# Block-sparse attention and a two-layer MLP on one core: one shared tile for the far keys of the first and last 32 queries, K copies on three engines, finer steps, another order

## Chip, cores, metric

One core of one Trainium2 chip. The metric is device time in microseconds (us). TensorE is PE, its weight loads PEld, VectorE DVE, ScalarE ACT, GpSimd POOL, SyncE SP.

## What is computed

q, k and v are [4, 8, 768, 64] (batch, heads, sequence, head size), in float32. The 768 positions are 24 blocks of 32.

```python
scores = 0.125 * q @ k^T
mask   = |block_i - block_j| <= 1, or block_i or block_j is 0 or 23,
         or block_j in sampled_blocks[block_i]          # 3 random blocks per row block
attn   = softmax(where(mask, scores, -1e9))
x      = (attn @ v) as [3072, 512]                      # batch*seq, heads*64
h      = x @ w_in                                       # [512, 2048]
g      = h if h >= 1; 0 if h <= -1; else (h + 1)**2 / 4
out    = g @ w_out                                      # [2048, 512]
```

Query blocks 0 and 23 see all keys; every other block sees block 0, block 23, its own, its two neighbours and three sampled ones, 8 blocks or 256 keys (repeats masked by a zero V row).

## The kernel before

**Attention.** Two heads (e = 0, 1) make a pair; there are 4 batches of 4 pairs, written P(b, j). A pair has up to four rounds (`ROUNDS`, line 36). Rounds 1 to 3 hold 8 query blocks, two groups g of four; a block w of a group fills 32 partitions, its 256 keys the columns. Blocks 0 and 23 sit in round 1 with keys 0 to 255; the other 512 keys of these two blocks are round 0. Before the change round 0 is a full tile per head: the block list (0, 1, 2, 23) for both groups, of which only positions 0 and 3 are used later. Per round and head: `scores` (L295) into a PSUM bank, `top` (reduce_max, L306), `expo` (L323, L326), `turn` (four transposes, L332), `turn_copy` (L336, to SBUF as pt), `values` (L350), and per round `norm`. Round 0 is first copied out by `stash` (L300), since its exponential waits for the maximum over both rounds (`top_global`, L311 to L315). float32 scores and values show as two PE instructions per matmul.

**Gathers.** Sampled K blocks are copied in SBUF to kg, three 32-column copies per query block (`gather_k_sampled`, L238): on POOL, in the early ("wide") rounds those with slot 0 (`KD`) on DVE. The block numbers come from registers that an engine loads at its first use (`blocks`, L122). Sampled V blocks go to vb: the first of three by a DMA that SP issues (L261), two by POOL copies (L263) out of va, a pair's near V rows.

**MLP.** `wi` (w_in) and `w` (w_out) are turned from 64-bit words into two float32r parts by 16 conversions: `load` (raw, L167, one buffer), `size` (ACT, L172), `bits` (four DVE operations, L177 to L182), `high` (ACT, L74), `low` (DVE, L191). Conversions 8 to 15 are w_in, 0 to 7 w_out; w_out's parts are kept in DRAM and loaded again later (L455). Each half batch (8 in all) runs 16 steps fi: `l1` (L471 to L473) into h, Relu and Square (L477, L480), max (L483), `gh` (L74), `gl` (L492), `l2` (L499 to L501) into three banks oa, copied out by `o_copy` (L508).

**Order.** Every step is a function in one list, `plan`. The steps get due times from constants, but then `RANK` (line 576), a list with one number per step, replaces them: the steps are issued in its order, and with that the order on each engine and on SP's DMA queue. Rounds 0 to 2 of batch 0 come first, together with the w_in conversions ("wide": up to three spare banks); its round 3 and the pairs of batches 1 to 3 are mixed into the MLP. The first `l1` is at 132 us, the last value matmul at 767 us.

`TCOPY = (1,)`: for the later rounds ACT copies pt of head 1, DVE that of head 0. `TCOPYW = (0,)`: in the wide rounds ACT copies that of head 0. `GL1`: the fi of the first half whose gl POOL makes. `SUBP`: conversions whose `low` POOL makes.

Of the kernel before, what the change touches and what calls it, by code (L numbers as in the profile page):

```python
# [30 lines left out]

ROUNDS = (
# [8 lines left out]
def body(ctx, tc, qk_t, v_rows, v_near, v_last, sampled_blocks, moe_w_in, moe_w_out, near, ident, out):  # L41
# [39 lines left out]
    wi = cst.tile([128, 4, 2, FF], F32R, name="wi")  # L81

# [31 lines left out]

    def blocks(engine, which, i):

        if engine not in held:
            rows = [1] if engine is ENG.SP else [0] if engine is ENG.DVE else [0, 1]
            held[engine] = {}
            for w in rows:  # L120
                for i0 in range(0, NI, 11):
                    _, vals = nc.values_load_multi_w_load_instructions(  # L122
                        kv_at[:, i0:i0 + 11, w], engines=[engine], min_val=0, max_val=2 ** 15 - 1,
                        skip_runtime_bounds_check_because="three fields of five bits, packed on the chip")
                    for k, v in enumerate(vals):
                        held[engine][w, i0 + k + 1] = v
        return held[engine][which, i]
# [80 lines left out]
    def pair(b, j, s, q, wide, rounds=(0, 1, 2, 3)):  # L208
# [21 lines left out]
        def gather_k_sampled(r):  # L230
            kg, kt = gat.tile([128, 8, BLK * NR], F32, name="kg"), st["k"]
            st["kg", r] = kg
            for k0, i0, n in runs(r):
                for k in range(n):
                    eng, et = (nc.vector, ENG.DVE) if wide and k in KD else (nc.gpsimd, ENG.Pool)
                    v = blocks(et, 0, i0 + k)
                    for a in range(NR):
                        eng.tensor_copy(out=kg[:, k0 + k, 32 * a:32 * a + 32],  # L238
                                        in_=kt[:, bass.ds(field(v, a, NB - 1) * BLK, BLK)])
# [11 lines left out]
        def gather_v_sampled(r, engine):  # L251
            vb = st["vb", r]
            for k0, i0, n in runs(r):
                for k in range(n):
                    for a in range(NR):
                        if (a in (V_SPW if wide else V_SP)) is not (engine is ENG.SP):
                            continue
                        v = field(blocks(engine, 1, i0 + k), a, NB)
                        dst = vb[32 * a + 32:32 * a + 64, k0 + k]
                        if engine is ENG.SP:  # L260
                            Q_V.dma_start(out=dst, in_=v_near[b, j, BLK:2 * BLK, bass.ds(v, 1)].rearrange("p a d -> p (a d)"))  # L261
                        else:
                            nc.gpsimd.tensor_copy(out=dst, in_=st["va"][32:64, bass.ds(v, 1)].rearrange("p a d -> p (a d)"))  # L263
# [8 lines left out]

        def scores(r):
            for e in range(2):
                st["s", r, e] = bank(f"s{e}", wide, 3 * j + r)
            kt = st["k"]
            for g in range(2):
                for n in range(3 if r else 1):
                    for w in range(4):
                        i = ROUNDS[r][g][w]  # L280
                        for e in range(2):
                            es = slice(64 * e, 64 * e + 64)
                            c0, c1 = (0, 96, 160, 256)[n:n + 2]
                            if r == 0:
                                c0, c1, rhs = 0, 256, kt[es, 256 + 256 * g:512 + 256 * g]
                            elif is_global(r, g, w):
                                rhs = kt[es, c0:c1]
                            elif n == 0:
# [282 lines left out]
KD = (0,)  # L571
# [231 lines left out]
```

## Time and profile before

| | us |
|---|---|
| median of 3 runs | 922.78 (921.85 to 932.03) |
| the profiled execution | 922.26 |
| its span | 920.5 |
| PE busy / weight loads | 820.0 / 692.9 |
| DVE, ACT, POOL busy | 423.8, 408.6, 448.4 |
| mean granted TensorE clock | 0.937 of full |

Busy times are unions within the span; matmuls overlap, so a mean duration times a count exceeds the time that they take. A wait is named by the semaphore that came last. "Idle before" is the time in which the engine stood before that group, and behind the arrow stands what ended it.

### The profile page before, as it was taken

How to read it: one execution, taken by the hardware profiler on the slowest of the kernel's cores; microseconds unless marked ns; L12 is line 12 of the kernel's file. 1: busy time of each engine (PE TensorE's matmuls, PEld its weight loads, DVE VectorE, ACT ScalarE, POOL GpSimd, SP SyncE). 2: the span in 40 equal slices, each digit the busy share in tenths (PEclk: the TensorE clock that was granted, in tenths of full speed). 3: DMA queues.
4: the chain of work that ended last, by engine and by line, in shares of the span. 5: the costliest groups of instructions: out<-in, count | busy, mean ns of one | idle time of the engine just before them, and what ended most of it. 6: DMA issues, size and time to landing. Idle time of an engine off the chain costs nothing.

```text
span 920.5 us, 33588 instructions
## 1 busy us (share of the span) xinstructions
PE 820.0 (89%) x12000; PEld 692.9 (75%) x12000; DVE 423.8 (46%) x925; ACT 408.6 (44%) x800; POOL 448.4 (49%) x1720
## 2 busy tenths in 40 slices
PE   2576377588999999899999989999999999999997
PEld 1355255467788888788888878888888888899896
DVE  5586673566854444334343434434443443222222
ACT  1344343334654544444445435634454443434343
POOL 2999757556766777346373637454746400000000
PEclk7587597688999999999999999999999999999999
DMA  6666757676656365545355535545463313443432
GB/s 226 200 225 203 244 195 283 228 229 206 232 174 238 95 213 169 182 151 175 128 181 195 166 128 184 172 154 189 134 211 131 117 56 130 149 137 127 160 115 103
DMA packets 56955, 159.54 MB, mean 173 GB/s; under 512 B 10579, under 2 KB 21972, under 8 KB 54228
## 3 DMA queue, kind: packets, MB, share of 16 engines
q1 hardware_dynamic: 56788, 157.40, 51.1%
q8 instruction: 94, 1.54, 0.7%
q14 instruction: 73, 0.60, 0.2%
HBM read 142.68 MB, written 14.68 MB: 171 GB/s over the span
## 4 chain that ended last, share of the span: by engine, by line
PE 70%; DMA 16%; DVE 4%; SPq 4%; issue 3%; ACT 3%; POOL 0%; POOLq 0%; DVEq 0%; ACTq 0%
PE oa L499 9%; PE oa L501 8%; PE oa L500 8%; PE h L471 8%; PE h L473 7%; PE h L472 7%; PE o L350 7%; PE s L295 6%; DMA va<-in_v_near_dram 5%; PE t L332 5%; DMA raw<-in_moe_w_out_dram 3%; SPq L261 3%; DMA raw<-in_moe_w_in_dram 2%; DMA w<-wo_dram 1%; DMA out_dram<-ot 1%
## 5 line engine op out<-in xcount | busy, mean ns | idle before, releaser
L263 POOL COPY vb<-va 32x130 f32 x704 | 234.3, 333 | 132.9 <-PE o L350 82.1
L238 POOL COPY kg<-k 128x32 f32 x1008 | 209.4, 242 | 142.2 <-PE s L295 96.8
L499 PE MATMUL oa<-w,gh 128*128 128x512 f32 x384 | 162.1, 422 | 15.4 <-DMA w<-wo_dram 7.1
L471 PE MATMUL h<-xt,wi 128*128 128x384 f32 x448 | 162.7, 363 | 4.7 <-DVE r L483 4.6
L501 PE MATMUL oa<-w,gl 128*128 128x512 f32 x384 | 153.5, 400 | 0.4 <-POOL gl L492 0.4
L500 PE MATMUL oa<-w,gh 128*128 128x512 f32 x384 | 153.1, 399 | 0.2 <-DVE w L191 0.2
L472 PE MATMUL h<-xt,wi 128*128 128x384 f32 x448 | 153.0, 342 | 0.0
L473 PE MATMUL h<-xt,wi 128*128 128x384 f32 x448 | 152.9, 341 | 0.0
L477 ACT ACTIVATE r<-h,half_c 128x384 f32<-128x384 f32 x112 | 65.2, 582 | 170.9 <-PE h L473 170.5
L483 DVE SCALAR_TENSOR_TENSOR r<-r,h 128x384 f32<-128x384 f32 x112 | 61.8, 552 | 155.6 <-ACT r L480 155.3
L471 PEld LDWEIGHTS h<-xt,wi 128*128 128x128 f32 x448 | 85.8, 192 | 16.5 <-DVE r L483 7.1
L499 PEld LDWEIGHTS oa<-w,gh 128*128 128x128 f32 x384 | 73.6, 192 | 29.9 <-issue 6.8
L74 ACT CAST gh<-r 128x384 fp32r<-128x384 f32 x128 | 65.6, 512 | 65.8 <-DVE r L483 61.4
L492 DVE TENSOR_TENSOR gl<-r,gh 128x384 fp32r<-128x384 f32 x124 | 69.4, 561 | 46.4 <-ACT gh L74 46.0
L472 PEld LDWEIGHTS h<-xt,wi 128*128 128x128 f32 x448 | 86.3, 193 | 4.3
L501 PEld LDWEIGHTS oa<-w,gl 128*128 128x128 f32 x384 | 73.3, 191 | 17.9 <-POOL gl L492 0.8
L295 PE MATMUL s<-k,q 64*32 64x96 f32 (+2 forms) x3376 | 74.5, 265 | 13.4 <-DMA k<-in_qk_t_dram 6.0
L473 PEld LDWEIGHTS h<-xt,wi 128*128 128x128 f32 x448 | 86.0, 192 | 0.0
L326 ACT ACTIVATE p<-s,m 128x256 f32<-128x256 f32 x176 | 72.0, 474 | 30.0 <-DVE m L318 29.6
L350 PE MATMUL o<-va,pt 128*32 128x65 f32 x1408 | 66.2, 235 | 20.0 <-ACT pt L336 12.6
L332 PE MATMUL t<-idf,p 128*128 128x128 f32 x464 | 76.0, 288 | 8.4 <-DVE pt L336 3.7
L500 PEld LDWEIGHTS oa<-w,gh 128*128 128x128 f32 x384 | 73.7, 192 | 9.0 <-issue 1.2
(83 smaller groups left out, 1112.5 us busy)
## 6 DMA issues: line engine op xcount, KB each, us to landing
w<-wo_dram SPq DMA_DIRECT2D x112, 512.0 KB, 3.5
va<-in_v_near_dram SPq DMA_DIRECT2D x20, 1625.0 KB, 8.1
raw<-in_moe_w_in_dram SPq DMA_DIRECT2D x16, 512.0 KB, 4.7
raw<-in_moe_w_out_dram SPq DMA_DIRECT2D x16, 512.0 KB, 5.2
wo_dram<-w SPq DMA_DIRECT2D x16, 512.0 KB, 4.6
q<-in_qk_t_dram SPq DMA_DIRECT2D x20, 384.0 KB, 4.0
k<-in_qk_t_dram SPq DMA_DIRECT2D x20, 384.0 KB, 4.5
vn<-in_v_rows_dram SPq DMA_DIRECT2D x16, 390.0 KB, 4.0
```

The costliest lines, as they stand in the source:

```text
L238: eng.tensor_copy(out=kg[:, k0 + k, 32 * a:32 * a + 32], in_=kt[:, bass.ds(field(v, a, NB - 1) * BLK, BLK)])
L263: nc.gpsimd.tensor_copy(out=dst, in_=st["va"][32:64, bass.ds(v, 1)].rearrange("p a d -> p (a d)"))
L295: nc.tensor.matmul(out=st["s", r, e][32 * w:32 * w + 32, 256 * g + c0:256 * g + c1], lhsT=st["q"][es, i * BLK:(i + 1) * BLK], rhs=rhs, sta ...
L326: nc.scalar.activation(out=p[:, 256 * g:256 * g + 256], in_=st["s", r, e][:, 256 * g:256 * g + 256], func=AF.Exp, bias=st["m", r][:, e, g: ...
L332: nc.tensor.transpose(out=t[:, c * 128:(c + 1) * 128], in_=st["p", r, e][:, c * 128:(c + 1) * 128], identity=idf)
L350: nc.tensor.matmul(out=o[32 * w:32 * w + 32, e, gd], lhsT=st["pt", r, e][:, k:k + 32], rhs=rhs, start=start, stop=stop)
L471: nc.tensor.matmul(out=hv, lhsT=wi[:, j, 0, fs], rhs=x[:, 0], start=(j == 0), stop=False)
L472: nc.tensor.matmul(out=hv, lhsT=wi[:, j, 0, fs], rhs=x[:, 1], start=False, stop=False)
L473: nc.tensor.matmul(out=hv, lhsT=wi[:, j, 1, fs], rhs=x[:, 0], start=False, stop=(j == NP - 1))
L499: nc.tensor.matmul(out=o, lhsT=gh[:, ts], rhs=w[:, 0], start=(fi == 0), stop=False)
L500: nc.tensor.matmul(out=o, lhsT=gh[:, ts], rhs=w[:, 1], start=False, stop=False)
L501: nc.tensor.matmul(out=o, lhsT=gl[:, ts], rhs=w[:, 0], start=False, stop=(fi == NF - 1))
```

## The change

- Round 0 becomes one tile for both heads: only blocks 0 and 23 are computed, head 0 in column groups 0 and 3, head 1 in 1 and 2. So one bank, one stash, one reduce over 512 columns, one exponential, one turn and one copy where there were two. In round 1 head 1's blocks are permuted to match (`place`).
- `top_global` uses an additive mask (`other`, 0 or -3e38) in place of operations on 32 partitions.
- `gather_k_sampled` becomes `gather_k` per half round and engine: in the wide rounds slots 0 and 4 on DVE, 1 and 7 on ACT, the others on POOL. `gather_v_sampled` is split in half rounds as well. Registers are loaded in a step of their own, on ACT too.
- `TCOPY = (0, 1)`, `GL1 = (0, 1, 4, 12)`, `SUBP = (7,)`, and a new `RANK` of 3089 numbers (2989 before).

```diff
-    ((0, 1, 2, 23), (0, 1, 2, 23)),
+    ((), ()),
...
+    other = cst.tile([128, 4], F32, name="other")
...
+        nc.vector.memset(other, -3.0e38)
+        for w, eg in enumerate((0, 2, 3, 1)):
+            nc.vector.memset(other[32 * w:32 * w + 32, eg:eg + 1], 0.0)
...
+        def gather_k(r, part, which):
+            if part == 0 and which == 0:
+                new_k(r)
+            eng, et = ((nc.gpsimd, ENG.Pool), (nc.vector, ENG.DVE), (nc.scalar, ENG.Activation))[which]
+            for k, i in slots(r, part):
+                if which != (1 if wide and k in KD else 2 if wide and k in KA else 0):
+                    continue
+                v = blocks(et, 0, i)
+                for a in range(NR):
+                    (eng.copy if which == 2 else eng.tensor_copy)(out=st["kg", r][:, k, 32 * a:32 * a + 32],
+                                                                   in_=st["k"][:, bass.ds(field(v, a, NB - 1) * BLK, BLK)])
...
+        def place(r, e, g, w):
+            if r == 0:
+                return (0, None, None, 3)[w] if e == 0 else (1, None, None, 2)[w]
+            if r == 1 and e == 1:
+                return ((1, 0, 2, 3), (0, 1, 3, 2))[g][w]
+            return w
+
         def scores(r):
-            for e in range(2):
+            kt = st["k"]
+            for e in range(2 if r else 1):
                 st["s", r, e] = bank(f"s{e}", wide, 3 * j + r)
+            if r == 0:
+                for g in range(2):
+                    for w in (0, 3):
+                        for e in range(2):
+                            es, z, i = slice(64 * e, 64 * e + 64), place(0, e, g, w), (NB - 1) * (w // 3)
+                            nc.tensor.matmul(out=st["s", 0, 0][32 * z:32 * z + 32, 256 * g:256 * g + 256],
+                                             lhsT=st["q"][es, i * BLK:(i + 1) * BLK],
+                                             rhs=kt[es, 256 + 256 * g:512 + 256 * g], start=True, stop=True)
+                return
...
         def top_global():
...
+            a, m = st["a"], st["m", 1].rearrange("p e g -> p (e g)")
+            t = pr.tile([128, 5], F32, name="m0")
+            nc.vector.tensor_tensor(out=t[:, 0:4], in0=m, in1=other, op=ALU.add)
+            nc.vector.tensor_copy(out=t[:, 4:5], in_=a)
+            nc.vector.reduce_max(out=a, in_=t, axis=AX.X)
+            nc.vector.scalar_tensor_tensor(out=m, in0=other, scalar=a[:, 0:1], in1=m, op0=ALU.add, op1=ALU.max)
             nc.vector.tensor_single_scalar(out=a, in_=a, scalar=-SCALE, op=ALU.mult)
...
-                at(t - G["gs"], gather_k_sampled, r)
+                for part in range(2):
+                    for which in range(3 if wide else 1):
+                        at(t - G["gs"] + 2.0 * part + 0.01 * which, gather_k, r, part, which)
...
+    for engine, rows in ((ENG.Pool, (0, 1)), (ENG.SP, (1,))) + (((ENG.DVE, (0,)),) if KD else ()) + (((ENG.Activation, (0,)),) if KA else ()):
+        at(TC + 0.1, registers, engine, rows)
...
-KD = (0,)
+KD = (0, 4)
+KA = (1, 7)
...
-GL1 = (0, 4, 8, 12)
-SUBP = ()
-TCOPY = (1,)
+GL1 = (0, 1, 4, 12)
+SUBP = (7,)
+TCOPY = (0, 1)
```

What the new `RANK` does at the places that the prediction names, read by sorting the steps. On SP, ahead of the load of conversion 9: before, 20 gathers of V blocks, then va of pair 1 between them; after, va of pair 1 first, then 10 gathers. Between the loads of conversions 15 and 0: before, 16 gathers, q, k, vn, va and two small loads; after, 8 gathers, va and one small load. On ACT, ahead of size of conversion 9: one pt copy before, two after; on DVE ahead of its bits: none before, one after. From batch 1 on, the places of a pair's steps among the MLP's `l1` and `l2` are nearly the same; the pairs P(2, 0) to P(2, 2) come a little earlier.

## Rows read from the trace of the kernel before

**Rows 1.** Windows by stage: the stretch in us, its length, then busy us (and instructions) of each engine, the granted clock of TensorE as a share of full, the share of the DMA engines, and GB/s.

```profile
0.00:132.00 132.00, 72.44 (x2004) 53.57 (x2004) 88.92 (x216) 51.09 (x90) 94.04 (x331) 0.73 0.65 216
132.00:250.00 118.00, 92.62 (x1140) 76.57 (x1133) 71.26 (x121) 51.10 (x98) 76.23 (x235) 0.84 0.70 235
250.00:740.00 490.00, 479.80 (x7734) 406.65 (x7733) 212.83 (x493) 234.24 (x477) 278.10 (x1156) 0.99 0.50 165
740.00:920.00 180.00, 175.12 (x1134) 156.08 (x1132) 50.82 (x97) 72.19 (x136) 0.00 (x0) 1.00 0.37 125
```

The columns of engines are PE, PEld, DVE, ACT, POOL.

**Rows 2.** What PE waited for from 250 to 740 us: us in total, times, longest.

```profile
PE oa L499 <- DMA w<-wo_dram: 7.1, 4, 3.8
...
PE t L332 <- ACT pt L336: 0.5, 1, 0.5
```

**Rows 3.** Waits of all engines over the whole span, columns as before.

```profile
DVE cva L177 <- ACT cva L172: 45.1, 11, 9.4
...
ACT cva L172 <- DMA raw<-in_moe_w_in_dram: 39.8, 8, 9.0
...
ACT cva L172 <- DMA raw<-in_moe_w_out_dram: 27.7, 6, 8.2
```

**Rows 4.** The chain that ended last: its shares of the span by line, and one piece of it (start us, us).

```profile
by line: PE oa L499 9.3%; PE oa L501 8.3%; PE oa L500 8.2%; PE h L471 7.7%; PE h L473 7.0%; PE h L472 7.0%; PE o L350 6.9%; PE s L295 5.8%; DMA va<-in_v_near_dram 5.0%; PE t L332 4.9%; issue 3.1%; DMA raw<-in_moe_w_out_dram 2.8%; SPq L261 2
...
24.11 7.63 DMA va<-in_v_near_dram
```

**Rows 5.** Timeline of PE around a turn (start us, us, instruction).

```profile
437.58 0.39 PE L501 MATMUL oa<-w,gl 128*128 128x512 f32 x1
437.81 0.60 PE L332 MATMUL t<-idf,p 128*128 128x128 f32 x4
...
438.48 0.39 PE L500 MATMUL oa<-w,gh 128*128 128x512 f32 x1
```

**Rows 6.** Timeline of PE around the round-0 scores of a later pair, and the score instructions at work in the stretch 470.05 to 470.2 and in 470.3 to 470.4 (durations min/median/max in ns, first and last start in us).

```profile
469.44 0.40 PE L500 MATMUL oa<-w,gh 128*128 128x512 f32 x1
469.67 0.40 PE L501 MATMUL oa<-w,gl 128*128 128x512 f32 x1
470.00 1.09 PE L295 MATMUL s<-k,q 64*32 64x256 f32 x32
...
L295 PE MATMUL s<-k,q x8: 400/400/400, 470.0 to 470.0; 64*32 64x256 f32 x8
...
L295 PE MATMUL s<-k,q x16: 376/388/400, 470.0 to 470.3; 64*32 64x256 f32 x16
```

**Rows 7.** Groups of instructions on ACT from 250 to 740 us: line, operation, shapes, count, then busy us, mean ns of one, idle before.

```profile
L477 ACT ACTIVATE r<-h,half_c 128x384 f32<-128x384 f32 x76 | 44.3, 583 | 120.0 <-PE h L473 119.7
L480 ACT ACTIVATE r<-r 128x384 f32<-128x384 f32 x76 | 40.0, 526 | 2.0
L74 ACT CAST gh<-r 128x384 fp32r<-128x384 f32 x76 | 38.9, 512 | 40.6 <-DVE r L483 40.5
L336 ACT COPY pt<-t 128x512 f32<-128x512 f32 x42 | 24.7, 588 | 33.8 <-PE t L332 33.3
L323 ACT ACTIVATE p<-sg,a 128x512 f32<-128x512 f32 x22 | 15.7, 719 | 2.2 <-DVE a L315 2.2
L300 ACT COPY sg<-s 128x512 f32<-128x512 f32 x21 | 11.6, 589 | 7.9 <-PE s L295 7.9
```

**Rows 8.** Groups by shape over the whole span, columns as in the group above.

```profile
L238 POOL COPY kg<-k 128x32 f32 x1008 | 209.4, 242 | 142.2 <-PE s L295 96.8 <-DMA vb<-in_v_last_dram 16.7 <-DMA k<-in_qk_t_dram 13.0
...
L336 DVE COPY pt<-t 128x512 f32<-128x512 f32 x58 | 40.0, 689 | 58.8 <-PE t L332 58.5
...
L306 DVE TENSOR_REDUCE m<-sg 128x2 f32<-128x512 f32 x32 | 20.6, 678 | 5.9 <-ACT sg L300 5.9
...
L238 DVE COPY kg<-k 128x32 f32 x48 | 6.8, 194 | 7.8 <-issue 5.4 <-PE oa L295 2.0
```

**Rows 9.** DVE's register loads (durations min/median/max in ns, first and last start in us).

```profile
L122 DVEq TENSOR_LOAD <-kv_at x2: 2502/2622/2741, 7.3 to 10.1; - x2
```

**Rows 10.** The second conversion: DVE's, ACT's and SP's timelines (start us, us; in brackets the idle time before and what ended it), and the landing times of all raw loads in us.

```profile
38.23 0.71 DVE L177 TENSOR_SCALAR cva<-cva 128x1024 f32<-128x1024 f32 x1 [9.44 <-ACT cva L172]
...
37.07 1.12 ACT L172 ACTIVATE cva<-raw 128x1024 f32<-128x1024 f32 x1 [8.21 <-DMA raw<-in_moe_w_in_dram]
...
31.82 0.84 SPq L167 DMA_DIRECT2D raw<-in_moe_w_in_dram  x2
...
DMA to landing us min/median/max: 3.6/4.7/10.9
```

**Rows 11.** The first w: timelines of SP, DVE and PE, columns as in the group above.

```profile
120.16 5.00 SPq L261 DMA_DIRECT2D vb<-in_v_near_dram  x8
...
137.79 0.83 SPq L167 DMA_DIRECT2D raw<-in_moe_w_out_dram  x2
...
127.50 1.23 DVE L182 SCALAR_TENSOR_TENSOR cva<-raw,cva 128x1024 int32<-128x1024 int32 x1
...
166.70 0.79 PE L499 MATMUL oa<-w,gh 128*128 128x512 f32 x1 [6.14 <-ACT w L74]
```

**Rows 12.** The last operation of bits of all 16 conversions, and the copies of the outputs on ACT (durations in ns, first and last start in us).

```profile
L182 DVE SCALAR_TENSOR_TENSOR cva<-raw,cva x16: 1224/1226/1266, 18.7 to 246.5; 128x1024 int32<-128x1024 int32 x16
...
L508 ACT COPY ot<-oa x23: 570/587/593, 269.4 to 916.9; 128x512 f32<-128x512 f32 x23
```

More of the change, by code (lines that the diff above doesn't have):

```diff
@@ L113, in body, with registers @@
     held = {}
-    def blocks(engine, which, i):
[L117 to L127, printed above, removed]
+    def registers(engine, rows):
+        for w in rows:
+            for i0 in range(0, NI, 11):
+                _, vals = nc.values_load_multi_w_load_instructions(
+                    kv_at[:, i0:i0 + 11, w], engines=[engine], min_val=0, max_val=2 ** 15 - 1,
+                    skip_runtime_bounds_check_because="three fields of five bits, packed on the chip")
+                for k, v in enumerate(vals):
+                    held[engine, w, i0 + k + 1] = v
+    def blocks(engine, which, i):
+        return held[engine, which, i]
     def field(v, a, top):
@@ L228, in runs, with slots, new_k @@
                 k0 += n
[L230 to L239, printed above, removed]
+        def slots(r, part):
+            k0, i0, n = list(runs(r))[part]
+            return [(k0 + k, i0 + k) for k in range(n)]
+        def new_k(r):
+            st["kg", r] = gat.tile([128, 8, BLK * NR], F32, name="kg")
+        def gather_k(r, part, which):
[9 more added lines that the diff above has]
+                                                                   in_=st["k"][:, bass.ds(field(v, a, NB - 1) * BLK, BLK)])
         def load_va():
@@ L249, in gather_v, with gather_v_sampled @@
             Q_V.dma_start(out=vb[0:32, 0:total], in_=v_last[b, j, :, k:k + total])
-        def gather_v_sampled(r, engine):
+        def gather_v_sampled(r, part, engine):
             vb = st["vb", r]
[L253 to L263, printed above, removed]
+            for k, i in slots(r, part):
+                for a in range(NR):
+                    if (a in (V_SPW if wide else V_SP)) is not (engine is ENG.SP):
+                        continue
+                    v = field(blocks(engine, 1, i), a, NB)
+                    dst = vb[32 * a + 32:32 * a + 64, k]
+                    if engine is ENG.SP:
+                        Q_V.dma_start(out=dst, in_=v_near[b, j, BLK:2 * BLK, bass.ds(v, 1)].rearrange("p a d -> p (a d)"))
+                    else:
+                        nc.gpsimd.tensor_copy(out=dst, in_=st["va"][32:64, bass.ds(v, 1)].rearrange("p a d -> p (a d)"))
         def slot(r, g, quarter):
@@ L329, in turn @@
         def turn(r, e):
-            t = st["t", r, e] = bank("t", wide, 7 * j + 2 * r + e)
+            t = st["t", r, e] = bank("t", wide, 6 * j + max(2 * r - 1, 0) + e)
             for c in range(4):
@@ L379, in x_turn @@
         def x_turn(hf):
[L380 removed]
+            t = st["xt", hf] = bank("t", wide, 6 * j + 5)
             for k, (r, n) in enumerate((((1, 0), (2, 0), (2, 1)), ((3, 0), (3, 1), (1, 1)))[hf]):
```

50 lines of the change are left out of this document (23 added, 27 removed), and 301 rows, old and new, of the table RANK.

## The prediction

> **What bounds the kernel now.** I read the windows by stage first [rows 1]; they show two kernels in one. From 250 to 740 us PE is busy 479.8 of 490 us, and 175.1 of 180 us from there on, at a granted clock of 0.99 to 1.00: PE is the bound, and only PE time that goes shortens the run. In the first 250 us PE is busy 165 us (granted clock 0.73, then 0.84), DVE 160 and POOL 170: nothing is full, so waits and the order of the steps set the end. The waits of PE from 250 to 740 us [rows 2] confirm the first half: the longest entry is 7.1 us, for w. For the second half I read the waits of all engines [rows 3]: DVE stood 45.1 us before a conversion's first operation, since ACT's came late, and ACT's own stood 39.8 + 27.7 us for the raw weights. The chain of waits [rows 4] gives the va transfers 5.0% and the raw ones 2.8% and more.
>
> **PE: what goes and what only looks as if it did.** Per pair one of two round-0 tiles goes: four transposes, a stash, a 512-wide reduce, an exponential, a copy of pt, and 16 of 32 score instructions.
>
> Transposes: in the PE-bound stage a block of four stands between an L501 that starts at 437.58 and an L500 at 438.48 [rows 5], 0.90 us. Without a block between, two such steps are 2 x 0.23 = 0.46 us (469.44 to 469.67 is one, [rows 6]). A block costs 0.44 us of PE, not the 1.15 us of four times the page's mean, because matmuls overlap. Eleven pairs have their round 0 after 250 us (22 exponentials of sg, two a pair, [rows 7]), one more shortly before: 12 x 0.44 = 5.3 us. A second way: the chain gives L332 4.9% of 920.5 us [rows 4], 45 us for 512 transposes; 64 of these are 5.6 us. I take 5.3. The first four pairs I leave out, because PE waits there.
>
> Round-0 scores: the count halves and I book nothing. In the block of 32 [rows 6] exactly 8 instructions have started within the first 0.2 us and exactly 16 by 470.4: eight places of the array (two halves of the rows by four groups of columns) run side by side, four deep, 1.09 us or 0.27 us a layer. After the change head 0 uses column groups 0 and 3, head 1 groups 1 and 2: four places, and each still gets two key groups of two passes, four deep again. It is between 0 and half the block, 12 x 0.5 = 6 us of further gain; I take 0, because the depth is counted from the rows.
>
> Value matmuls keep number and shape, and the permuted heads of round 1 still fill four different column groups: 0.
>
> **DVE, ACT, POOL.** A later pair takes from DVE a reduce (0.68 us) and four pt copies (0.69 each), 3.4 us [rows 8]. ACT loses a stash (0.59) and an exponential (0.72) and gains three pt copies net (0.59 each): +0.45 us [rows 7], where it is busy 234 of 490 us. PE covers both: 0; with that cover gone ACT's part would cost 12 x 0.45 = 5 us. The new top_global is five small operations for six; its 5-wide reduce, which no row shows, lies between nothing and the 0.68 us of a 512-wide one, and is hidden in the same way, as are five memsets while DVE waits for the block list.
>
> K copies: with KD = (0, 4) and KA = (1, 7) POOL loses five blocks of three copies per early pair (two in round 1, three in round 2), 60 copies at 0.242 us [rows 8], 14.5 us of the 94 that it is busy in the first 132. I do not add this to the sum: it is what lets POOL follow when the order gets faster. On ACT 36 small copies appear that the trace lacks; between DVE's 0.19 us and the 0.59 us of a 512-wide ACT copy they take 7 to 21 of the 81 us that ACT is idle there. I take 0.2 to 0.25 each, as on the two engines that show such a copy. DVE gets 24 copies, 4.7 us, and loses 4 x (0.68 + 0.69) = 5.5: even.
>
> Register loads: ACT gets two TENSOR_LOADs ahead of its first stash. DVE has its own two until 12.6 us [rows 9] ahead of the reduce that reads the stash, so a stash that moves from 8 to 12 us is not late: 0, at worst 2 us. SP's loads only move behind va of pair 1, on the same queue. Conversion 7's two subtractions and POOL's four gl change engine or place among idle POOL time: 0, at worst 2 us for the last w. Half rounds as steps add no instruction; they only allow the order.
>
> **The order: two waits that I see go.** I sorted the steps by the new list.
>
> The first [rows 10]: DVE stands 9.44 us until 38.23, ACT 8.21 until 37.07, for the raw of conversion 9. SP issued it at 31.82 us, when the buffer had been free since 18.7 + 1.2 = 19.9 us (the first L182, [rows 12]): ahead of it stood 20 gathers and va of pair 1, and SP went on only when that va had landed (24.11 + 7.63 us, [rows 4]). In the new order ten gathers precede it and va goes out ahead of them all, so it can leave at about 20 us and land 4.7 us later. Pair 0's first pt copies now also precede that conversion on ACT and DVE, so its values no longer queue behind it. I book the 9.4 us. Late next are POOL's vb copies for pair 0, which now start nine blocks of K copies earlier (27 x 0.242 = 6.5 us).
>
> The second [rows 11]: PE stands 6.14 us until 166.70 for the first w of the first MoE half. Its raw (conversion 0) left at 137.79 us, though the buffer was free at 127.50 + 1.23 = 128.7: between the two raws SP had 16 gathers, q, k, vn and va. Now it has 8 gathers and one va. Eight gathers take 5.0 us there and q, k and vn some 1.3, so 6.3 us go, and with them the 6.1. I book 6.1.
>
> Sum: 5.3 + 9.4 + 6.1 = 20.8 us. The profiled execution took 922.26 us (span 920.5), 0.5 under the median of the runs, 922.78; 922.8 - 20.8 = 902.0.
>
> What the order is worth beyond that has wide ends: all sixteen conversions pass one raw buffer, 15.2 us apart on average (first L182 at 18.7, last at 246.5, [rows 12]), and a new wait may also eat what I booked.
>
> **Rivals.** (A) *More waits go than I name.* If three quarters of DVE's 45.1 us for conversions go [rows 3], the 9.4 among them, that is 34 us, and with 5.3 us of PE 883. For it: POOL's 14.5 us, and loads that are issued earlier throughout. Against it: the DMA engines are busy 0.65 to 0.70 of the time already [rows 1], and a raw takes 3.6 to 10.9 us to land [rows 10].
>
> (B) *The order gives nothing*: the transfers keep the first 250 us at their length and other waits replace the two. Only the transposes remain: 917.5.
>
> (C) *Two heads in one bank do not run side by side.* Now the two row halves write two banks, after the change one. If they took turns, four deep would become eight, up to 1.0 us more per pair: 12 x 1.0 = 12 us, 914. No row shows two halves in one bank. Against it: they write different partitions of it.
> The Trainium skill speaks against the change here: TensorEngine Tiling (Array Packing), Restrictions and Gotchas, says "Different row tiles cannot access same PSUM bank simultaneously". By that rule the time is (C)'s, by the depth counted in [rows 6] mine.
>
> (D) *Slower: ACT becomes the queue that PE waits for.* ACT now makes both heads' pt copies, and the later pairs have one t bank, so a second turn cannot start until ACT has copied the first. Found behind Relu, Square and the cast to gh (0.58 + 0.53 + 0.51 = 1.62 us, [rows 7]), a copy waits half of that on average, 0.81 us; on 4 x 12 copies that is 39 us: 902 + 39 = 941. It turns the sign above 0.43 us a copy (20.8 / 48), and is slower by 1% above 0.62. Against it: 42 copies for the other head are on ACT there already, and PE waited for such a copy 0.5 us in all [rows 2].
>
> That the change does not do what it says holds for the time of the scores; it is in the sum as 0.
>
> **How the numbers follow.** Forecast 0.47 (own range 890 to 912), A 0.20, B 0.18, C 0.07, D 0.06, the rest 0.02. The range 884 to 920 holds the forecast, B, C and half of A. A measurement of this kernel tells about 1%, 9 us, from no change. Faster is below 913.6: the forecast, A, half of C, less a little for the forecast's edge, 0.72. B and the rest of C are same, 0.20; D and the unnamed slower, 0.08.
>
> **What would show it.** Transposes down to 448 at L332, and L332's part of the chain down by some 5 us. Blocks of 16 round-0 scores that still take about 1.1 us (right), 0.6 us (more gain) or 2 us (C). No idle DVE stretch of 9 us before 40 us, the wait for cva under 35 us, no 6 us wait for the first w. The first output copy, now at 269.4 us [rows 12], some 15 us earlier, and from it to the end 5 us less. I am wrong if that copy stays where it is (B), or if PE waits for ACT's pt by over 20 us in the later stage (D).

## The result and the profile after

The changed kernel takes 867.34 us (865.35 to 869.64, four runs), beside 924.61 for the kernel before: ratio 0.937, 95% interval 0.931 to 0.943. Forecast were 902.0 us, with a range of 884 to 920. The sign was right; the gain is 57 us, not 21. The profiled execution took 866.1 us, span 864.3.

Windows by stage of the changed kernel (columns as in [rows 1]), cut at the first `l1`, at the first output copy and at 690 us. The first stretch ends at the same step as that of [rows 1]; the second does not, since there the first output copy comes at 269.4 us and the cut is at 250:

```profile
0.00:113.00 113.00, 62.66 (x1829) 47.69 (x1830) 77.41 (x203) 48.03 (x113) 86.88 (x269) 0.80 0.74 246
113.00:240.00 127.00, 109.94 (x1606) 91.37 (x1606) 82.77 (x141) 70.41 (x136) 105.66 (x327) 0.96 0.78 258
240.00:690.00 450.00, 447.65 (x7144) 382.46 (x7143) 167.24 (x404) 223.46 (x462) 258.48 (x1093) 1.00 0.53 171
690.00:864.00 174.00, 169.34 (x1105) 150.99 (x1104) 48.23 (x93) 70.82 (x134) 0.00 (x0) 1.00 0.39 128
```

PE's busy time sums to 789.6 of 864 us, before to 820.0 of 920 [rows 1]: 26 us less idle and 30 less busy. By an estimate from these rows most of the 30 is the clock: busy time times the missing share of the clock is 72.4 x 0.27 + 92.6 x 0.16 + 479.8 x 0.01 = 39 us before and 62.7 x 0.20 + 109.9 x 0.04 = 17 after. That leaves some 8 us for work that went.

The last operation of bits of the 16 conversions, the copies of the outputs on ACT, and the waits around the conversions (answering to [rows 12] and [rows 3]):

```profile
L186 DVE SCALAR_TENSOR_TENSOR cva<-raw,cva x16: 1224/1226/1265, 18.5 to 223.3; 128x1024 int32<-128x1024 int32 x16
...
L543 ACT COPY ot<-oa x23: 565/586/632, 239.9 to 860.8; 128x512 f32<-128x512 f32 x23
```

```profile
DVE cva L181 <- ACT cva L176: 27.9, 14, 6.1
...
ACT cva L176 <- DMA raw<-in_moe_w_in_dram: 15.6, 5, 6.2
ACT cva L176 <- DMA raw<-in_moe_w_out_dram: 10.0, 5, 5.8
```

The first output copy comes 29.5 us sooner (269.4 to 239.9), and from it to the last one it is 620.9 us instead of 647.5: two nearly equal halves of the gain. From the first output copy to the last, in the kernel before, with the shared tile alone in the old order (x1, below) and in the changed kernel:

```profile
269.40:916.90 647.50, 635.52 (x8615) 546.33 (x8613) 252.60 (x564) 295.98 (x592) 265.71 (x1110) 0.99 0.46 153
267.80:914.10 646.30, 630.90 (x8411) 540.89 (x8409) 244.66 (x544) 278.64 (x562) 265.24 (x1110) 0.99 0.46 154
239.90:860.80 620.90, 617.09 (x8249) 533.55 (x8247) 215.47 (x497) 293.82 (x597) 258.58 (x1094) 1.00 0.49 159
```

Here PE's idle time falls from 12.0 to 3.8 us and its busy time by 18.4. The tile takes 204 instructions and 4.6 us of busy time. A further 162 instructions (14 large products, 96 score, 48 value and 4 transposing ones) the new order does before the first output instead of behind it: some 6 us, an estimate at 0.2 us for a large product, 1.3 us for 79 scores and 1.0 us for 48 values in the timelines. So some 6 us of the second half are work that moved into the first.

Over the whole span ACT waits 25.6 us for raw weights where it waited 67.5, and the conversions are 13.7 us apart instead of 15.2.

What PE waited for from 240 to 690 us (answering to [rows 2]):

```profile
PE o L380 <- issue: 1.2, 1, 1.2
PE oa L534 <- ACT r L512: 0.8, 1, 0.8
PE s L321 <- POOL kg L250: 0.2, 1, 0.2
```

The 7.1 us for w, which the prediction left standing, are gone.

The second conversion in the changed kernel, on DVE, ACT and SP (answering to [rows 10]):

```profile
32.08 0.69 DVE L181 TENSOR_SCALAR cva<-cva 128x1024 f32<-128x1024 f32 x1 [0.97 <-ACT cva L176]
...
30.85 1.20 ACT L176 ACTIVATE cva<-raw 128x1024 f32<-128x1024 f32 x1 [2.63 <-DMA raw<-in_moe_w_in_dram]
...
25.40 0.84 SPq L171 DMA_DIRECT2D raw<-in_moe_w_in_dram  x2
```

DVE's 9.44 us are 0.97, and its first step comes 6 us sooner.

### The profile page after: what moved, and what is told of

It is laid out like the page before. It is cut to its first block, busy times and chain, and to the rows that moved or that the text cites. A ratio compares the mean times of both kernels' runs of the same rounds, so it can differ in the third digit from the quotient of the medians.

```text
span 864.3 us, 32912 instructions
## 1 busy us (share of the span) xinstructions
PE 789.6 (91%) x11680; PEld 672.5 (78%) x11680; DVE 375.7 (43%) x840; ACT 412.7 (48%) x844; POOL 451.0 (52%) x1686
## 4 chain that ended last, share of the span: by engine, by line
PE 71%; DMA 8%; issue 6%; POOL 4%; DVE 3%; ACT 3%; POOLq 2%; SPq 2%; DVEq 1%; ACTq 0%
PE oa L534 9%; PE oa L536 9%; PE oa L535 8%; PE h L506 8%; PE h L508 7%; PE h L507 7%; PE o L380 6%; PE s L321 5%; PE t L362 4%; DMA va<-in_v_near_dram 3%; DMA raw<-in_moe_w_out_dram 3%; POOL vb L274 2%; POOL kg L250 1%; PE s L508 1%; PE s L506 1%
## 5 line engine op out<-in xcount | busy, mean ns | idle before, releaser
L274 POOL COPY vb<-va 32x130 f32 x704 | 242.9, 345 | 155.7 <-PE o L380 110.7
L250 POOL COPY kg<-k 128x32 f32 x972 | 200.5, 238 | 65.6 <-PE s L321 33.9
L506 PE MATMUL h<-xt,wi 128*128 128x384 f32 x448 | 159.5, 356 | 5.0 <-DVE r L518 5.0
L534 PE MATMUL oa<-w,gh 128*128 128x512 f32 x384 | 160.5, 418 | 3.3 <-issue 2.4
L508 PE MATMUL h<-xt,wi 128*128 128x384 f32 x448 | 151.7, 339 | 0.0
L507 PE MATMUL h<-xt,wi 128*128 128x384 f32 x448 | 151.7, 339 | 0.0
L535 PE MATMUL oa<-w,gh 128*128 128x512 f32 x384 | 150.4, 392 | 0.3 <-DVE w L195 0.3
L506 PEld LDWEIGHTS h<-xt,wi 128*128 128x128 f32 x448 | 84.9, 189 | 15.7 <-DVE r L518 6.3
L507 PEld LDWEIGHTS h<-xt,wi 128*128 128x128 f32 x448 | 85.1, 190 | 4.5
L534 PEld LDWEIGHTS oa<-w,gh 128*128 128x128 f32 x384 | 72.3, 188 | 16.2 <-issue 4.2
L508 PEld LDWEIGHTS h<-xt,wi 128*128 128x128 f32 x448 | 84.9, 189 | 0.0
L362 PE MATMUL t<-idf,p 128*128 128x128 f32 x416 | 66.6, 284 | 15.5 <-ACT p L353 10.3
L535 PEld LDWEIGHTS oa<-w,gh 128*128 128x128 f32 x384 | 72.5, 189 | 7.6 <-DVE w L195 0.7
L366 ACT COPY pt<-t 128x512 f32<-128x512 f32 x96 | 56.3, 586 | 35.7 <-PE t L362 35.6
L362 PEld LDWEIGHTS t<-idf,p 128*128 128x128 f32 x416 | 50.7, 144 | 28.5 <-ACT p L353 11.6
```

What stands on the lines that cost most here:

```text
L250: (eng.copy if which == 2 else eng.tensor_copy)(out=st["kg", r][:, k, 32 * a:32 * a + 32], in_=st["k"][:, bass.ds(field(v, a, NB - 1) * BL ...
L362: nc.tensor.transpose(out=t[:, c * 128:(c + 1) * 128], in_=st["p", r, e][:, c * 128:(c + 1) * 128], identity=idf)
L506: nc.tensor.matmul(out=hv, lhsT=wi[:, j, 0, fs], rhs=x[:, 0], start=(j == 0), stop=False)
L507: nc.tensor.matmul(out=hv, lhsT=wi[:, j, 0, fs], rhs=x[:, 1], start=False, stop=False)
L508: nc.tensor.matmul(out=hv, lhsT=wi[:, j, 1, fs], rhs=x[:, 0], start=False, stop=(j == NP - 1))
L534: nc.tensor.matmul(out=o, lhsT=gh[:, ts], rhs=w[:, 0], start=(fi == 0), stop=False)
```

## The experiments

Each was timed beside the kernel before, which lay between 924.6 and 927.2 us; ratios are to it, with 95% intervals.

### One part at a time, in either order

The old order in these runs is the new code with its steps at the places that the old list gave them.

> The changed kernel's shared tile alone, in the old order: its steps stand where the old kernel's order had them, the K copies go to VectorE and GpSimd in the old slots and none to ScalarE, and the three small settings of the expert layers are the old ones. The kernel before is at 922 to 925 us, the changed one at 867. Theory O (most of the 57 us comes from the new order: 26 us less waiting on TensorE and 22 us less of its work at half clock): only the transposes and the few instructions go, 916 to 922 us. Rival T (the shared tile shortens the chain of each head pair in the wide stage, and that gives most): 880 to 895 us. Rival K (three engines at the K copies give most): as O here, 916 to 922 us.

> Every part of the change but the order: shared tile, K copies on three engines, half rounds as steps, the three small settings, all at the places that the old kernel's order had. Theory O: 908 to 918 us (GpSimd does 36 copies of 242 ns less, 8.7 us, of which in the old order little lies on TensorE's path). Rival K: under 890 us. Rival T: 875 to 890 us.

> The changed kernel in its new order, but with the K copies split as before (VectorE two slots of a wide round, GpSimd the rest, ScalarE none): GpSimd does 36 copies more than in the changed kernel, 8.7 us by 242 ns. Theory O: 868 to 876 us, since GpSimd is nearly always busy in the first 130 us of the changed kernel and a part of the 8.7 us shows there. Rival K: 885 us or more. Rival T: 867 to 870 us.

> The changed kernel with the three small settings as before: the low halves of the first expert half on GpSimd for steps 0, 4, 8 and 12 instead of 0, 1, 4 and 12, no weight remainder on GpSimd instead of that of the last w_out conversion, and only the second of the two narrow turn copies on ScalarE instead of both. Theory O (the order made for one set of settings and the sequence of steps do the work; the settings only fit it): 867 to 872 us. Rival (the settings themselves are a large part): 876 us or more.

> The new order and the shared tile alone: K copies split as before and the three small settings as before. Measured so far: the changed kernel 867 to 869 us, without the K split 875.4, with the old settings 880.7, the shared tile in the old order 919.9. Theory O (the order is the cause, and split and settings add 8 and 13 us by themselves): 886 to 892 us. Rival S (the order is worth its gain only with the settings and the split that it was made for): 898 us or more.

> The old order with the shared tile and the K copies on three engines, but the three small settings as before. The old order with the tile alone is at 919.9 us, with split and settings at 930.6. Theory T (the settings cost the 11 us there: both turn copies stand in ScalarE's queue, and TensorE's transposes wait 21 us in all for that copy from 139 to 288 us): 918 to 922 us, since what GpSimd no longer copies it waits for loads. Rival K (the copies on ScalarE cost it): 927 to 931 us.

> The changed kernel with one of the three small settings undone: of the two narrow turn copies only the second on ScalarE, the first back on VectorE. Theory T (the turn copy in VectorE's queue stands behind the four steps of a weight conversion, and TensorE waits for it, as in the run with all three settings undone: 4.2, 5.4, 1.3 and 4.0 us): 876 to 881 us. Rival (the low halves on GpSimd make the difference): 867 to 870 us.

```diff
# old order: RANK of the same steps from the old list        (x1, x3, q3)
# old split:                                                  (x1, x4, q2)
-KA = (1, 7)
+KA = ()
-if which != (1 if wide and k in KD else 2 if ...
+if which != (1 if wide and k in ((0, 3) if r == 1 else KD) else 2 if ...
# old settings:                                               (x1, x7, q2, q3)
-GL1 = (0, 1, 4, 12); SUBP = (7,); TCOPY = (0, 1)
+GL1 = (0, 4, 8, 12); SUBP = ();   TCOPY = (1,)
# q1: TCOPY = (1,) alone
```

Measured, all with the shared tile:

| | old order | new order |
|---|---|---|
| old split, old settings | x1 919.9 (0.989 to 0.998) | q2 882.2 (0.951 to 0.957) |
| new split, old settings | q3 914.3 (0.985 to 0.993) | x7 880.7 (0.944 to 0.953) |
| old split, new settings | not run | x4 875.4 (0.943 to 0.954) |
| new split, new settings | x3 930.6 (1.002 to 1.008) | 867.3 (0.931 to 0.943) |

The shared tile alone brings 5 us: theory O held, rival T fell. The order alone brings 38 more (q2 against x1), better than O's 886 to 892. With the new split, the three settings cost 16 us in the old order (x3 against q3) and bring 13 in the new one (the changed kernel against x7). In the new order q1 (879.9 us, 0.943 to 0.953) shows that one of them, the turn copy, carries this; in the old order no run undoes it by itself, and only the waits below point to it. In the new order split and settings also need each other: the split brings 1.5 us with the old settings (x7 against q2), which is within the noise, and 8 with the new ones (the changed kernel against x4); the settings bring 7 with the old split (x4 against q2) and 13 with the new. O gave x3 908 to 918 and x7 867 to 872; both are wrong, and x7's rival held. K and T, which gave x3 890 or less, are wrong too. In q3's terms the settings cost it and not the copies on ScalarE: 914.3 us is 4 us better than even that forecast. By the medians q3 is 6 us under x1, but the two intervals overlap.

What PE waited for from 132 to 300 us in x3 and then from 100 to 250 us in q1:

```profile
PE t L362 <- ACT pt L366: 17.4, 5, 6.7
PE o L380 <- ACT pt L366: 5.6, 2, 5.3
```

```profile
PE t L362 <- DVE pt L366: 13.1, 4, 4.6
PE t L362 <- ACT w L75: 3.5, 1, 3.5
```

A turn must wait until the copy of the one before has freed its bank. In the old order that copy stands late in ACT's queue, in the new one it would stand late in DVE's; from 100 to 250 us the changed kernel has 2.4 us of turns waiting for a copy. These settings are right only for one of the two orders.

### The loads' places in SyncE's queue

> The shared tile alone in the old order (920 us when it ran), but with the loads, the row fetches and the weight loads on SyncE's queue in the changed kernel's sequence for the first 130 us or so; TensorE, ScalarE, VectorE and GpSimd keep the old one. Theory L (GpSimd's copies set the first 130 us: 94 us of work in the 115 us from 17 to 132 before, with 13.8 us of waiting for k and the value rows, and ScalarE stands 34 us there for raw weights; the loads' places in SyncE's queue cause these waits): most of the new order's gain comes back, 893 to 907 us. Rival E (the places of the work on the computing engines themselves do it, as ScalarE's first pass of a conversion no longer standing ahead of copies that others wait for): 915 to 922 us.

> The changed kernel with the steps of SyncE's queue (loads, row fetches, weight loads) in the old sequence for the first 140 us or so, all else in the new order. Theory L: most of the gain goes, 890 to 907 us. Rival E: 867 to 878 us. The prediction's own sum (two waits of 9.4 and 6.1 us by the sequence of two loads): 876 to 884 us.

> The changed kernel with one thing of the old order back: on SyncE's queue the raw weights of the second conversion go out behind the second pair's value rows and its first 12 row fetches, as before. The prediction's first wait by itself, undone. By the prediction's sum 9.4 us come back, 876 to 877 us. Theory L (GpSimd sets this stage, and ScalarE and VectorE have slack beside it): under half of it, 868 to 872 us. Theory C (a wait and the half clock behind it): over 877 us.

> The changed kernel with one thing of the old order back: the row fetches of pair 1's last half stand behind the load of the last w_in conversion, and the loads of pair 3's q and k and the next batch's value rows ahead of the load of the first w_out conversion. The prediction's second wait by itself, undone. By the prediction's sum 6.1 us come back, 873 to 874 us. Theory C (a wait costs its length and the half clock behind it): 874 to 878 us. Rival: TensorE's order here (sixteen more first-layer products and pair 3's scores ahead of the second second-layer group) hides the later weights, 866 to 869 us.

```diff
# y1, y2: RANK merged from both lists, SP's steps from the one, all others from the other
# x5:
+MOVE = {11: 47.5, 66: 57.2, 36: 57.4}   # va of pair 1, 4 fetches, raw of the 2nd conversion
# x6:
+MOVE = {287: 317.1, 290: 317.2, 308: 317.3, 349: 317.4, 351: 317.5, 379: 317.6, 305: 317.7}
+RANK = tuple(MOVE.get(r, r) for r in RANK)
```

y1 913.2 us (0.981 to 0.991): the loads' places alone bring 7 us over x1. In y1 two of the loads go a little earlier than the new list has them. y2 887.9 us (0.955 to 0.963): with them back in the old places the changed kernel loses 20 of its 52 us over x1. Neither theory holds: y1 lies between L's 893 to 907 and E's 915 to 922, nearer E's; y2 lies just under L's 890 to 907 and above the prediction's 876 to 884. The loads' places and the engines' own queues work together, and by the medians the new loads bring 7 us without the new queues, split and settings and 20 with them.

x5 874.1 us (0.939 to 0.948): 7 us by the medians, between L's and the prediction's numbers, though the interval overlaps with the changed kernel's. Its output copies:

```profile
L543 ACT COPY ot<-oa x23: 567/587/634, 240.7 to 868.6; 128x512 f32<-128x512 f32 x23
```

The second conversion is 5 us later there, but the first output only 0.8 (240.7 instead of 239.9). So the 7 us are lost behind the first output, where PE has a wait that the changed kernel lacks:

```profile
PE oa L534 <- ACT ot L543: 3.4, 2, 2.3
```

What ties this wait to the late raw weights, no run shows; the first wait by itself is not the direct price of the 7 us.

x6 880.1 us (0.944 to 0.955): 13 us, more than any of the three theories expected, and in another way. POOL's timeline in x6 (start us, us, in brackets idle and what ended it):

```profile
105.17 9.50 POOL L250 COPY kg<-k 128x32 f32 x36
127.95 5.26 POOL L274 COPY vb<-va 32x130 f32 x16 [13.28 <-DMA va<-in_v_near_dram]
133.27 2.38 POOL L250 COPY kg<-k 128x32 f32 x12
```

PE's wait in x6 from 113 to 150 us:

```profile
PE s L321 <- POOL kg L250: 15.4, 1, 15.4
```

The edit puts va of pair 1 behind these loads as well. The late va holds POOL for 13.3 us, the next pair's K copies stand behind it, and PE waits 15.4 us for these, not for w. With va earlier the same wait is 6.7 us. So x6 prices that va, and the prediction's second wait by itself stays without a price.

### The late weights and the half clock

> The kernel before with 15 of its 112 loads of second-layer weights moved ahead of the row fetches that stand between the moment their buffer is free and them on SyncE's queue; nothing else is changed. The prediction took these waits (7.1 us of TensorE from 250 to 740 us) as staying. If they go and cost their length alone: 6 to 7 us, 918 to 920 us. Theory C (their length and the half clock behind them, 3.3 and 3.5 us of busy time at half clock behind the two longest): 8 to 11 us, 914 to 918 us. Rival: the row fetches, now later, are waited for instead, 923 to 926 us.

> The kernel before, with 117 extra transposes of the identity into columns that nobody reads, put ahead of five waits of TensorE: 38 of them in the 6.1 us at 160.6 us, 21 in the 3.5 us at 176.8, 19 in the 3.1 us at 201.6, 24 in the 3.8 us at 381.1, 15 in the 2.5 us at 536.0. At 0.15 us each they end inside the wait. After these waits TensorE's records of before show half clock (163 to 173, 180 to 187, 204 to 210, 385 to 388, 538 to 542 us), with some 25 us of busy time in them. Theory C (a wait costs its length and then the half clock after it, in a stage that TensorE bounds): the waits stay but the half clock goes, 909 to 917 us, though work was added. Rival N (the half clock is paid in time that TensorE would have waited anyway): 921 to 926 us, and more by whatever filler overruns its wait.

```diff
# p3, on the kernel before: 15 w loads to where their buffer is free
+MOVE = {831: 796.1, 906: 877.1, 933: 898.1, 999: 974.1, ...}
+RANK = tuple(MOVE.get(r, r) for r in RANK)
# d1, on the kernel before: ahead of five turns, values or l2 steps
+    for _ in range(FILL.get((kind, calls[kind]), 0)):
+        nc.tensor.transpose(out=spare["o"][:, 384:512], in_=idf, identity=idf)
```

p3 913.4 us (0.982 to 0.991): 9 to 17 us for waits of 7.1. Its PE waits from 250 to 740 us, and the same window by engines:

```profile
PE t L332 <- ACT pt L336: 1.3, 1, 1.3
...
PE oa L499 <- DMA w<-wo_dram: 0.8, 1, 0.8
```

```profile
250.00:740.00 490.00, 486.62 (x7825) 413.29 (x7825) 214.74 (x498) 236.47 (x482) 276.75 (x1156) 1.00 0.50 167
```

From the first output copy to the last (the kernel before stands in the section on the result):

```profile
269.30:906.40 637.10, 632.29 (x8616) 544.74 (x8615) 252.79 (x565) 295.76 (x593) 264.44 (x1110) 1.00 0.47 156
```

Theory C holds here: the clock is back at 1.00, and more went than the waits' length. In the profiled executions this stretch is 10.4 us shorter, 7.2 of them idle time of PE and 3.2 busy time, with the same work; the first output copy stays where it was. The median, 913.4 us, lies just under C's 914 to 918.

d1 920.95 us (0.992 to 0.998): 2 to 7 us, less than C's 8 to 16 and at the edge of N's 921 to 926. From the first product behind the waits at 160, 381 and 536 us on, first before and then d1:

```profile
166.70:173.00 6.30, 6.14 (x15) 4.87 (x16) 2.61 (x5) 1.03 (x2) 5.61 (x16) 0.51 0.99 281
385.00:388.00 3.00, 3.00 (x10) 2.62 (x11) 0.58 (x1) 1.10 (x3) 0.00 (x0) 0.51 0.63 239
538.00:542.00 4.00, 3.54 (x18) 2.72 (x22) 0.45 (x1) 0.00 (x1) 0.00 (x0) 0.57 0.55 217
```

```profile
168.16:174.46 6.30, 5.90 (x21) 4.88 (x22) 2.59 (x5) 1.03 (x2) 5.65 (x18) 0.73 0.99 280
389.80:392.80 3.00, 2.99 (x18) 2.64 (x19) 0.69 (x1) 2.03 (x5) 0.00 (x0) 1.00 0.82 331
538.70:542.70 4.00, 4.00 (x66) 3.26 (x65) 0.56 (x1) 1.07 (x2) 0.00 (x0) 1.00 0.38 149
```

The clock is at or near the lower level (0.5) behind these waits. With filler in them it stays up behind the two late ones. Behind the three before 250 us, where 1.5 to 2.4 us of wait are left without filler, it comes back only in part (0.73 here, 0.76 and 0.72 behind the other two). From the first `l1` to the first output d1 takes as long as before (138.3 and 137.4 us in the profiled executions); behind it, it gains:

```profile
273.40:914.80 641.40, 636.07 (x8654) 548.54 (x8651) 252.82 (x564) 295.77 (x593) 264.37 (x1110) 1.00 0.46 155
```

There 39 transposes of filler (4.6 us) raise PE's busy time by only 0.6 us over the 635.5 of before: 4 us of half clock went. So behind the first output the half clock is paid. Before it, what came back of the clock bought nothing, since PE then waits for other engines; a run with the full clock there is missing. So not all of the 22 us of clock in the account above need be a cause: where PE waits for others, it can be a symptom.

### The raw buffer

> The shared tile alone in the old order (919.9 us), with the same edit: two raw buffers, one each of the other two tiles, each load of raw weights from the third conversion on at the place of the one before it. ScalarE of the kernel before waits 67.5 us for raw weights. Theory V (in the old order that wait, with the loads behind row fetches on SyncE's queue, sets the spacing of the conversions, 15.2 us against 13.7 in the new order): 900 to 911 us. Rival G: 914 to 922 us.

> The changed kernel with two buffers for the raw weights of a conversion in place of one (and one each for the conversion's second tile and for the stashed far scores, to make room), and from the third conversion on each load of raw weights at the place of the one before it on SyncE's queue. Theory V (16 weight conversions run one after another through the single raw buffer, and the first half's output follows the last of them by 16.3 us in every run of the new order so far, by 22 to 24 us in every run of the old one; ScalarE still waits 25.6 us for raw weights): the conversions come closer together, the last one 5 to 15 us sooner, 855 to 863 us. Rival G (VectorE's and ScalarE's queues and GpSimd's copies pace the conversions anyway): 865 to 872 us.

```diff
-RAWB, CVAB = 1, 2
+RAWB, CVAB = 2, 1
-st["sg"] = pr.tile([128, 512], F32, name="sg")
+st["sg"] = pr.tile([128, 512], F32, name="sg", bufs=1)
# and from the third conversion on, load n at the place of load n - 1
```

d6 899.8 us (0.969 to 0.976): 20 us over x1, a little better than theory V's range. z5 870.7 us (0.934 to 0.946): nothing, as rival G said. The last operation of bits, and the outputs, in x1, then d6, then z5:

```profile
L186 DVE SCALAR_TENSOR_TENSOR cva<-raw,cva x16: 1224/1225/1266, 18.6 to 245.9; 128x1024 int32<-128x1024 int32 x16
...
L543 ACT COPY ot<-oa x23: 566/586/593, 267.8 to 914.1; 128x512 f32<-128x512 f32 x23
```

```profile
L186 DVE SCALAR_TENSOR_TENSOR cva<-raw,cva x16: 1224/1225/1264, 18.6 to 227.4; 128x1024 int32<-128x1024 int32 x16
...
L543 ACT COPY ot<-oa x23: 566/587/604, 249.6 to 891.2; 128x512 f32<-128x512 f32 x23
```

```profile
L186 DVE SCALAR_TENSOR_TENSOR cva<-raw,cva x16: 1224/1242/1268, 18.2 to 223.5; 128x1024 int32<-128x1024 int32 x16
...
L543 ACT COPY ot<-oa x23: 567/587/634, 240.2 to 864.0; 128x512 f32<-128x512 f32 x23
```

d6's ACT waits 13.5 us for raw weights (x1's 72.2), z5's 5.9. In the old order the last conversion comes 18.5 us sooner for it than in x1, and the first output 18.2. In the new order taking away 20 of the 25.6 us that ACT still waits buys nothing: the last conversion stays at 223. The edit also leaves cva one buffer in place of two, and in z5 ACT waits 3.3 us for that buffer, which it does not in the changed kernel; so z5 is what is left of the two. Most simply read, the new order had already taken the wait for raw weights off the path.

### One more wait

> The changed kernel with 36 more K copies taken from GpSimd and given to ScalarE (slots 1 and 2 of a wide first round, 1, 3, 5 and 7 of a wide second round, in place of 1 and of 1 and 7). Theory G (GpSimd, busy 87 of the 96 us from 17 to 113 in the changed kernel, sets the time to the first expert product): 36 times about 240 ns is 8.7 us less on it, of which most shows, 858 to 863 us. Rival A (ScalarE's queue has taken its place, or its later copies hold back what others wait for): 865 to 871 us.

> The changed kernel with the gather of the first round's K ahead: VectorE's and ScalarE's share stands before the first conversion's steps, and GpSimd loads the registers for K, gathers K, and only then loads those for V. TensorE's 11.3 us of waiting at 9.0 to 20.4 us should be 4 to 6 us shorter. Theory G (GpSimd's total sets this stage): its work is the same and only put in another sequence, 864 to 868 us. Rival F (the first wait is on the path that sets the end): 860 to 863 us.

> The changed kernel with one step moved on GpSimd's queue: the K copies of the second part of pair 2's last round ahead of the 16 V copies of pair 1's last half, which stand between 114.3 and 122.4 us. TensorE waits 6.7 us for these K copies from 117.2 us. If that wait is on the path: 6 us less and up to 3 us of half clock behind it, 858 to 862 us. Rival (given back at the next conversion or at the end of the first half, as the 3 us that the 36 copies taken from GpSimd gained by the first expert product were): 865 to 869 us.

```diff
# z2, in gather_k
+KA = {1: (1, 2), 2: (1, 3, 5, 7), 3: ()}     # KA[r]
# z1: registers(POOL, (0,)) first, (1,) at the first V copy
+MOVE = {21: 16.8, 28: 16.9, 24: 17.1, 26: 17.2, 22: 17.3}
# z4
+MOVE = {341: 327.9}
```

z2, z1 and z4 took 869.7, 869.1 and 868.4 us (0.936 to 0.943, 0.934 to 0.941, 0.937 to 0.941): no gain in any. Theory G gave z2 858 to 863; its rival held, as z4's did, and rival F of z1 did not (theory G's 864 to 868 missed z1 by 1 us). z2 and z1 reach the first `l1` 3 us sooner (109.2 and 110.0 us instead of 112.7). z1 has lost it by the first output (241.2 us), z2 keeps it to there (237.0 instead of 239.9) and loses it behind. What PE waited for from 113 to 150 us, in the changed kernel and then in z4:

```profile
PE s L321 <- POOL kg L250: 6.7, 1, 6.7
PE h L506 <- DVE r L518: 3.3, 2, 2.3
PE t L362 <- ACT pt L366: 0.7, 1, 0.7
```

```profile
PE h L506 <- DVE r L518: 8.9, 3, 4.6
PE t L362 <- ACT pt L366: 3.5, 1, 3.5
```

The 6.7 us go and come back as 5.6 and 2.8 for DVE and ACT. Theory G, that POOL sets this stage, is not borne out: 36 copies fewer (z2), 8.7 us of POOL's time, move the first output by 3 us and the end not at all. No engine is full in the first 240 us of the changed kernel; POOL, the busiest, works 192.5 of them. What paces the conversions there, 13.7 us apart, these runs leave open.

## Why the prediction was wrong

**Transposes, 5.3 us: right.** L362 has 416 + 32 = 448 of them, as forecast. x1, with the tile alone, gains 2 to 10 us, and behind the first output its PE is busy 4.6 us less. Of that only 1.2 us show in this stretch of its profile, since its waits for w there grow from 7.1 us:

```profile
PE oa L534 <- DMA w<-wo_dram: 11.2, 6, 2.5
```

**Round-0 scores, 0 us: right.** A block of 16 in the PE-bound stage of the changed kernel:

```profile
255.31 1.07 PE L301 MATMUL s<-k,q 64*32 64x256 f32 x16
```

Half the instructions take the 1.09 us of [rows 6]. Rival C's 2 us, and with it the sentence of the Trainium skill's TensorEngine Tiling (Array Packing), Restrictions and Gotchas, do not show where two row halves write different partitions of one bank.

**K copies, booked as leeway: wrong in count and in sum.** The old split tested the slot within each part, so DVE already had two slots a round (its 48 copies in [rows 8]). POOL lost 1008 - 972 = 36 copies, not 60. Nor did DVE get 24 more: it makes 48 before and after. The new split is worth 8 us in the new order with the new settings (x4), and with the old settings 6 in the old order (q3) and 1.5 in the new (x7), neither of which is clear of the noise.

**The turn copies, booked at nothing under PE's cover: wrong.** I looked for the cover from 250 us on. Rival D's mechanism is real, but earlier and tied to the order: in the old one the settings cost 16 us (x3), turns and values wait 23.0 us for ACT's copies from 132 to 300 us, and x3 is slower than before. In the new order the turn copy alone brings the 13 us (q1).

**The order: this step failed.** It booked two waits that I could see go, 9.4 and 6.1 us, and let all others stand. The order alone is worth 38 us (q2 against x1), and with the split and the settings that were made for it 52.
- The first wait: the raw of the second conversion now leaves at 25.4 us, not at 20, and DVE waits 0.97 us for ACT there. By itself it is worth 0.8 us at the first output (x5), not 9.4; at the end x5 is 7 us slower, by waits that no run ties to it. It stood for a whole kind: in the old order the waits for raw weights together are worth 20 us (d6), and a second buffer or the new order takes most of them away. Rival A (883) named this kind, and its place and sign were right. Its size was not: DVE's wait for cva fell by 17.2 us (45.1 to 27.9), not by 34, and the time came under 883 through what A did not name, the waits for w and the settings.
- The second wait is gone too, but I had misread whose it was. In the kernel before, six groups of three products with w start from 152.66 to 157.30 us, before the one at 166.70 of [rows 11]. The first conversion of w_out had given two w at 149.30; the third, for which PE waits, is that of the second conversion, whose raw SP issues at 153.32, not at 137.79. And x6 shows that va, a neighbour in the queue, holds PE up there, through POOL. The lines of PE, ACT and SP:

```profile
152.66 0.39 PE L499 MATMUL oa<-w,gh 128*128 128x512 f32 x1
...
157.30 0.39 PE L499 MATMUL oa<-w,gh 128*128 128x512 f32 x1
...
149.30 1.14 ACT L74 CAST w<-cva 128x512 fp32r<-128x512 f32 x2 [1.57 <-DVE cva L182]
...
153.32 0.81 SPq L167 DMA_DIRECT2D raw<-in_moe_w_out_dram  x2
```

- The 7.1 us for later weights [rows 2] I read as staying, since they were short. Taken away in the old kernel they bring 9 to 17 us (p3).
- I saw granted clocks of 0.73 and 0.84 [rows 1] and gave them no price. What they cost before the first output stays open (d1); behind it, half clock was worth 3 to 4 us (p3, d1).

These do not add up to 57 and need not: 5 (x1), 20 (d6) and 13 (p3), each measured by itself in the old order, make 38. No run has them together. The split and the settings bring 15 us in the new order (the changed kernel against q2). How much of the rest belongs to the engines' own places, no run separates.

Of the marks that I had set, five came true (448 transposes, blocks of 1.07 us, no idle DVE stretch of 9 us before 40 us, the wait for cva under 35 us, no 6 us for the first w) and the size of three did not: the transposes' part of the chain fell from 4.9% of 920.5 us to 4.0% of 864.3, some 10 us and not 5; the first output came 29.5 us sooner, not 15; and behind it 27 us went, not 5. One sum was off as well: the chance of 0.72 for faster is more than its own terms, 0.47 + 0.20 + 0.035.

## What to carry to other kernels

When a new order moves hundreds of steps, price the kinds of wait that it can reach (all waits of one engine for one queue), not the few that can be followed by hand, and let the kind's whole sum set the range's end. A setting that says which engine makes a copy has no price of its own: the same three settings, with the turn copy among them, cost 16 us in one order and brought 13 in the other, so try a setting in the order it is meant for. In a stage that TensorE bounds, a short wait costs more than its length (7.2 us of idle time took 3.2 us of busy time with it in p3); in a stage where it waits anyway, a wait that goes may come back as another (z4).

## What the runs showed of the hardware

- Behind a wait of 3.8 us the granted clock is 0.51 over 385 to 388 us, behind one of 2.5 us 0.57 over 538 to 542; with transposes of no use in the wait it is 1.00 over the same length behind both.
- ScalarE's copies of 128 x 32 elements, for which I had no row, take 235 ns each in the mean (36 of them) in the changed kernel, as long as GpSimd's 238 (972) and longer than VectorE's 191 (48); my estimate of 200 to 250 holds.
- ScalarE's TENSOR_LOAD of registers took 2.5 us in the changed kernel; those of the other engines took 2.3 to 2.7.
